# A second layer in column passes of 512 and 256 instead of 384 and 384, and more of the output stored in whole rows

## The chip, the core and the metric

The kernel runs on one core of a Trainium2 chip. The core has a matrix engine (TensorE, "PE" in the profile, with its weight loads as "PEld"), a vector engine (VectorE, "DVE"), an activation engine (ScalarE, "ACT"), a general engine (GpSimd, "POOL"), and SyncE ("SP"), whose queue issues all DMA transfers here. Sixteen DMA engines carry them. PE writes its results into PSUM; ACT or DVE copies them to SBUF; DMA moves SBUF to and from HBM. The metric is the device time of one execution in microseconds (us): 370.72 us before the change, the median of three runs (370.67 to 371.68).

## What is computed

Attention with a sigmoid in place of a softmax, for 8 batches, 12 heads, 448 tokens and head size 64, and behind it a soft mixture of experts on the 3584 tokens x 768 columns that come out (all float32):

```
attn = sigmoid(q k^T / 8 - log 448);  x = (attn v), heads side by side          # 3584 x 768
logits = x phi                                                                  # 3584 x 32 slots
d = softmax over the tokens;  slot_input = d^T x                                # 32 x 768, 4 slots for each of 8 experts
h = max(slot_input[e] w1[e], 0);  slot_out[e] = h w2[e]                         # w1: 8 x 768 x 1024, w2: 8 x 1024 x 768
c = softmax over the slots;  out = c slot_out                                   # 3584 x 768
```

w1 and w2 are 25.2 MB each, the output is 11.0 MB. The change concerns the last two lines only: the second layer (w2), the combination with c, and the stores of the output.

## The kernel before, in words

**Attention and slots.** The first part runs over batches and pairs of heads, with the weights' first units loaded beside it. It ends with the slot inputs (`sT`). Tokens of each batch may be held in another order on the chip: `token_of` (L819) says which token stands at which place, and the queries are permuted on the host by it. Output rows are then stored in that order.

**Weights.** w1 and w2 lie in HBM as 128 units of 128 partitions x 768 columns (0.39 MB each): units 0 to 63 are w1, 64 to 127 are w2. `load_unit`, `load_units` and `load_pair` bring units 0 to 71; `reload` (L128) brings units 72 to 127 into buffers that have become free: `reload(i)` for i from 0 to 9 loads four units with one DMA into `wq0` to `wq9` (units 72+4i to 75+4i), `reload(11)` three into `wa`, `reload(12)` four and then three into `y1`, `reload(13)` three behind `yw[1]`, `reload(14)` two and then one into `xv`. They are called in that order, two behind each expert's first layer (`w1_part`, L669), and all are issued on SP's queue ahead of every store. `units` and `utile` say which tile holds which unit.

**Second layer.** It goes over the output columns in two passes (`hf`), 384 columns (`HALF`) each. One pass has 16 steps (`w2_step`, L775, two for each expert), each with four matmuls of [128 x 32]^T by [128 x 384] into four column groups of PE, all accumulated in one PSUM tile `po`. A unit holds two such blocks of 384 columns; so pass 0 reads w2 units 0 to 31 (units 64 to 95) and pass 1 reads w2 units 32 to 63 (units 96 to 127). Before each expert's two steps GpSimd copies its h into a zeroed buffer (L780). Between the steps of pass 0 stands the softmax over the slots (`combine`, L683).

**Combination.** After a pass `gather` (L758) copies the four partial sums from PSUM in two parts, `spread_sum` (L764) adds them up with a matmul by a constant matrix and copies the sum (`st`), and `out_job` (L710) multiplies it with c. The 28 row blocks of 128 tokens are divided in eight jobs of four and three blocks: job k does blocks of batch pair r = k//2. Each block is a matmul [32 x 128]^T by [32 x 384] (L729; up to four blocks at once in the four row groups of PE), and a copy to SBUF by ACT or DVE in turn (L740). PE's order is written out by hand: in pass 1, `spread_sum` of pass 0 stands before step 3, and out job n-4 before step n, for n = 4 to 11 (L808 to 813). After pass 1, gather, spread and all eight jobs follow for the second half of the columns, in the order 2, 3, ..., 7, 0, 1.

**Stores.** Of the 28 blocks, 16 are stored in two parts, after each pass its 384 columns (rows of 1.5 KB; L743 and L746, five DMAs after each pass); 12 are stored after the second pass in whole rows, two tokens on one partition (6 KB; L751, six DMAs). The staging tiles are `wq` buffers that the first pass has used up.

Of the kernel before, what the change touches and what calls it, by code (L numbers as in the profile page):

```python
# [9 lines left out]
F32 = mybir.dt.float32  # L10
# [14 lines left out]
NPR = H // 2  # L25
NKC = DM // P
NFC = F // P
HALF = DM // 2
UNIT = 768
N_Q = 10  # L30
N_B = 15
N_1 = 4 * N_Q + 17 + N_B
N_T = 4 * N_Q + 3
W_X = N_1 - N_B
NCH = 7
QW = 2 * S
NP = B * NPR
WARM = 6
# [3 lines left out]
BLK = 32  # L42
# [23 lines left out]
def soft_moe_attention(ctx: ExitStack, tc: tile.TileContext, qk, v, vl, phi, wu, wd, wq, wt, cst, out):  # L66
    nc = tc.nc
    ctx.enter_context(tc.manual_schedule(engines=MANUAL))

    wpa = ctx.enter_context(tc.tile_pool(name="wpa", bufs=1))  # L70
    small = ctx.enter_context(tc.tile_pool(name="small", bufs=1))

    places, k = {}, 0
    for name, w in (("cst", 2 * P), ("bias", 1), ("mz", 3), ("rz", 1), ("sm", SLN + 2 * T1),
                    ("phi", NKC * NSLOT), ("lt", B // 2 * NCH * BLK)):
        places[name] = slice(k, k + w)
        k += w
# [9 lines left out]
    nc.vector.memset(nbias, -math.log(S))  # L87

    units = [("w1", e, q, kh) for e in range(E) for kh in range(2) for q in range(4)]
    units += [("w2", hf, e, g, y) for hf in range(2) for e in range(E) for g in range(2) for y in range(2)]  # L90
    state = {"next": 0, "more": N_1}
    utile = {}
    quads = [wpa.tile([P, 4, UNIT], F32, name=f"wq{i}") for i in range(N_Q)]
# [2 lines left out]
    qx = wpa.tile([P, 3, UNIT], F32, name="qx")  # L96
    yt = [wpa.tile([P, 2, 4, TR, NCH, BLK], F32, name=f"y{i}") for i in range(2)]
    yw = {}

    def late_unit(k):  # L100
        return wpb.tile([P, UNIT], F32, name=f"wb{k}")[:]

    def load_units(ns, dst):
        for k, n in enumerate(ns):
            t = wb[n - W_X - 3] if dst is None else dst[:, k, :]
            nc.sync.dma_start(t, wu[n])
            utile[units[n]] = t
# [20 lines left out]
    def reload(i):  # L128
# [31 lines left out]
    with ExitStack() as actx:  # L160
# [12 lines left out]
        first = [("qk", 1), ("qk", 2), ("vl", ""), ("v", 1), ("att0", ""), ("att1", ""), ("xy", "")]  # L173
# [358 lines left out]
        for r in range(NP // 2):  # L532
            p = 2 * r
# [20 lines left out]
        for q, bs in enumerate(jobs):  # L554
            u = (bs[-1] + 1) * per_b + LAG
# [4 lines left out]
            if bs[-1] >= B - 3:  # L560
                k = bs[-1] - B + 3
                at(late, u + 2, lambda k=k: take_y(k))
                n = N_T + 4 + 3 * k
                for i, w in enumerate(((4, 8, 12), (2, 3, 5))[k]):
                    at(late, u + w, lambda k=k, n=n + i, i=i: load_units([n], yw[k][:, 4 + i:5 + i, :]))
            rate.update({u - 2: 1, u - 1: 1, u: 0, u + 1: 0, u + 2: 1, u + 3: 1.2, u + 5: 0.6, u + 6: 1.2})
        for i in range(2):
            at(late, u + 6 + 2 * i, lambda i=i: load_units([N_1 - 2 + i], yw[1][:, 2 + i:3 + i, :]))
        at(late, u + SLOT_AT - 1, lambda: load_units(range(N_1 - 4 - N_B, N_1 - 1 - N_B), xv[:, 0:3, :]))
        at(late, u + SLOT_AT, lambda: slot_job(len(jobs) - 1))  # L570
        at(late, u + SLOT_AT + 1, lambda: load_units(range(4 * N_Q, 4 * N_Q + 4), yw[0][:, 0:4, :]))
# [2 lines left out]
        i = seq.index((NP - 2, NFK - 1)) + LAG  # L574
# [5 lines left out]
        todo = deque()  # L580
# [10 lines left out]
        for i in range(len(seq) + LAG):  # L591
            for f in early.get(i, ()):
                f()
            if i < len(seq):
                u = seq[i]
# [26 lines left out]
            if i >= LAG:  # L622
                u = seq[i - LAG]
# [5 lines left out]
                p, c = u  # L629
# [20 lines left out]

    wpb = ctx.enter_context(tc.tile_pool(name="wpb", bufs=1, reuse_waits="tile"))
    hc = sm[:, 0:E * 32].rearrange("p (e f s) -> p e f s", e=E, f=NFC)
    tmp = sm[:, E * 32:E * 32 + HALF]
    ps_t = ctx.enter_context(tc.tile_pool(name="ps_t", bufs=4, space=PSUM, reuse_waits="tile"))
    ps_h = ctx.enter_context(tc.tile_pool(name="ps_h", bufs=1, space=PSUM, reuse_waits="tile"))
    ps_o = ctx.enter_context(tc.tile_pool(name="ps_o", bufs=2, space=PSUM, reuse_waits="tile"))
# [50 lines left out]
    def psum(n):  # L707
        return ps_t.tile([P, 512], F32, name="pt") if n % 3 else ph_tile(n // 3 + 1)

    def out_job(k, hf):  # L710
        r, o = divmod(k, 2)
        if o == 0 and r == 0:
            w = wpa.tile([P, 4 * UNIT], F32, name=f"wq{8 * hf}")
            halves[0] = w[:, 0:NCH * HALF].rearrange("p (j c) -> p j c", j=NCH)
        elif o == 0:
            if hf == 0:
                rows[r] = wpa.tile([P, 4, UNIT], F32, name=f"wq{r}")
            if r < 3:
                state["wh"] = wpa.tile([P, 2, 2 * UNIT], F32, name=f"wq{4 + 2 * hf + r // 2}")
            halves[r] = state["wh"][:, r % 2, 0:3 * HALF].rearrange("p (j c) -> p j c", j=3)  # L720
        hc = slice(hf * HALF, (hf + 1) * HALF)
        copies = (nc.scalar.copy, nc.vector.tensor_copy)
        todo = []
        for c in range(4 * o, 4 + 3 * o):
            pf = psum(state["out"])
            state["out"] += 1
            n = NCH * r + c
            g = slice(32 * (n % 4), 32 * (n % 4) + 32)
            nc.tensor.matmul(  # L729
                pf[:, 0:HALF], flat[g, P * (n // 4):P * (n // 4 + 1)], sts[hf][g, :], start=True, stop=True)  # L730
            todo.append((c, pf))
        t0 = NCH * P * r
        for i, (c, pf) in enumerate(todo):
            if r == 0:
                ov = halves[0][:, c, :]
            elif 2 <= c < 5:
                ov = halves[r][:, c - 2, :]
            else:
                ov = rows[r][:, c if c < 2 else c - 3, hc]
            copies[i % 2](ov, pf[:, 0:HALF])  # L740
            if r == 0 and c in (3, 6):
                j = slice(0, 4) if c == 3 else slice(4, 7)
                nc.sync.dma_start(  # L743
                    out[j.start * P:j.stop * P, hc].rearrange("(j p) c -> p j c", p=P), halves[0][:, j, :])
            elif r and c == 4:
                nc.sync.dma_start(  # L746
                    out[t0 + 2 * P:t0 + 5 * P, hc].rearrange("(j p) c -> p j c", p=P), halves[r])
            elif r and hf == 1 and c in (1, 6):
                j = 0 if c == 1 else 2
                to = t0 + (0 if c == 1 else 5 * P)  # L750
                nc.sync.dma_start(  # L751
                    out[to:to + 2 * P, :].rearrange("(p k) c -> p k c", k=2), rows[r][:, j:j + 2, :])

    cms, sts, rows, halves = {}, [], {}, {}
    spare = phi_flat
    state["out"] = 0

    def gather(po):  # L758
        so = tmp
        nc.scalar.copy(so[:, 0:HALF // 2], po[:, 0:HALF // 2])  # L760
        nc.scalar.copy(so[:, HALF // 2:], po[:, HALF // 2:HALF])
        return so

    def spread_sum(so):  # L764
        if not sts:
            state["st"] = late_unit(1)
        st = state["st"][:, len(sts) * HALF:(len(sts) + 1) * HALF]
        for k, copy in enumerate((nc.scalar.copy, nc.vector.tensor_copy)):
            c = slice(k * HALF // 2, (k + 1) * HALF // 2)
            pr = ps_t.tile([P, 512], F32, name="pt")  # L770
            nc.tensor.matmul(pr[:, 0:HALF // 2], rep, so[:, c], start=True, stop=True)  # L771
            copy(st[:, c], pr[:, 0:HALF // 2])  # L772
        sts.append(st)

    def w2_step(po, hf, n):  # L775
        e, g = divmod(n, 2)
        h = hw[e % 2]
        if g == 0:
            o = NSLOT - SPE
            nc.gpsimd.tensor_copy(  # L780
                h[:, o:o + NFC * NSLOT].rearrange("p (f s) -> p f s", f=NFC)[:, :, 0:SPE], hc[:, e])
        for fl in range(4):
            k = (4 * g + fl) * NSLOT + NSLOT - SPE - SPE * e
            ut = utile[("w2", hf, e, g, fl // 2)][:, fl % 2 * HALF:(fl % 2 + 1) * HALF]
            nc.tensor.matmul(  # L785
                po[32 * fl:32 * fl + 32, 0:HALF], h[:, k:k + NSLOT], ut,
                start=(n == 0), stop=(n == 2 * E - 1))

    prev = (0, ph)
# [35 lines left out]


# [43 lines left out]
```

## Time and profile before

| | |
|---|---|
| device time, median of 3 runs | 370.72 us (370.67 to 371.68) |
| profiled execution: span, first to last instruction | 369.5 us (no other time of it is given; the median lies 1.2 us above its span) |
| PE busy | 345.6 us, 94% of the span |
| DVE, ACT busy | 214.2 us, 217.9 us |
| mean DMA rate | 258 GB/s over the span, 95.25 MB |
| HBM written | 11.01 MB |
| chain that ended last | PE 81%, DMA 13% of the span |

The time is that of the whole execution; the profile shows one execution with an instruction-by-instruction record. The shares are averages over stages with different limits, so the stage in which the change lies, the last 70 us or so, has to be read by itself: which engine is busy there, which transfers are under way, and who waits for whom. Times within the span count from its start. A DMA's "time to landing" runs from its issue on SP's queue to its end.

### The profile page before, as it was taken

The numbers are of one execution on the slowest core, as the hardware profiler recorded it, in microseconds if no ns is written. First come the engines' busy times: TensorE is split into PE (matmuls) and PEld (weight loads), VectorE is DVE, ScalarE is ACT, GpSimd is POOL, SyncE is SP. The second block draws the span as 40 slices with busy tenths as digits, with TensorE's granted clock in tenths as the row PEclk, the third lists the DMA queues.
The fourth block names the chain that finished last, engine by engine and source line by source line (L and its number), as shares of the span: only waits on it lengthen the run. The fifth ranks groups of instructions, "written<-read, shape, count | busy, mean of one in ns | idle before, by whom it ended". The sixth has DMA issues, their size and how long they took to land.

```text
span 369.5 us, 9946 instructions
## 1 busy us (share of the span) xinstructions
PE 345.6 (94%) x4167; PEld 161.8 (44%) x4167; DVE 214.2 (58%) x482; ACT 217.9 (59%) x294; POOL 5.1 (1%) x24
## 2 busy tenths in 40 slices
PE   9999999999999999999999999999999979997810
PEld 5455555533343354434333633453457643322600
DVE  0155849199764926995764499969855344141510
ACT  5777777587777765777777487747673001142610
POOL 0000000000000000000000000000000001100000
PEclk9999999999999999999999999999999998999975
DMA  7675766667766683676767176429999999999997
GB/s 244 219 225 188 256 219 228 191 184 223 227 210 233 196 271 88 212 233 221 236 217 222 36 227 201 130 64 309 335 317 327 431 421 426 423 419 407 393 407 296
DMA packets 35548, 95.25 MB, mean 258 GB/s; under 512 B 3760, under 2 KB 17712, under 8 KB 33712
## 3 DMA queue, kind: packets, MB, share of 16 engines
q1 hardware_dynamic: 35504, 94.62, 73.2%
q8 instruction: 33, 0.54, 0.6%
q14 instruction: 11, 0.09, 0.1%
HBM read 83.59 MB, written 11.01 MB: 256 GB/s over the span
## 4 chain that ended last, share of the span: by engine, by line
PE 81%; DMA 13%; ACT 0%; DVE 0%; issue 0%; ACTq 0%
PE sc L237 35%; PE av L286 33%; DMA wq<-in_wq_dram 7%; DMA xv<-in_wt_dram 6%; PE sc L329 3%; PE sc L402 2%; PE pt L729 2%; PE ph L155 1%; PE av L155 1%; PE av L527 1%; PE av L266 1%; PE av L409 0%; PE ph L729 0%; PE pt L771 0%; PE po L785 0%; PE av L319 0%
## 5 line engine op out<-in xcount | busy, mean ns | idle before, releaser
L244 ACT ACTIVATE att<-sc,keep 128x896 f32<-128x896 f32 (+1 forms) x167 | 167.4, 1003 | 69.0 <-PE sc L237 64.4
L237 PE MATMUL sc<-qk 64*64 64x448 f32 x896 | 114.5, 536 | 0.0
L303 DVE STREAM_TRANSPOSE y<-xv 32x384 f32<-32x384 f32 (+5 forms) x144 | 69.2, 481 | 2.4
L286 PE MATMUL av<-att,xv 64*64 64x448 f32 x576 | 69.1, 536 | 0.0
L286 PE MATMUL av<-att,v 64*64 64x448 f32 x552 | 65.9, 536 | 0.0
L237 PEld LDWEIGHTS sc<-qk 64*64 64x64 f32 x896 | 41.3, 133 | 45.2 <-issue 18.7
L237 PE MATMUL sc<-qx 64*64 64x448 f32 (+1 forms) x448 | 60.4, 538 | 0.0
L303 DVE STREAM_TRANSPOSE y<-qx 32x288 f32<-32x288 f32 (+5 forms) x80 | 36.0, 450 | 1.3
L286 PEld LDWEIGHTS av<-att,xv 64*64 64x64 f32 x576 | 21.7, 131 | 32.7 <-ACT att L244 30.0
L293 DVE TENSOR_TENSOR xv<-xv,av 128x448 f32<-128x448 f32 x24 | 14.9, 621 | 35.6 <-ACT xv L289 17.6
L286 PEld LDWEIGHTS av<-att,v 64*64 64x64 f32 x552 | 20.5, 131 | 31.3 <-ACT att L244 30.7
L237 PEld LDWEIGHTS sc<-qx 64*64 64x64 f32 x448 | 20.8, 136 | 21.5 <-issue 10.0
L303 DVE STREAM_TRANSPOSE y<-xy 32x288 f32<-32x288 f32 (+1 forms) x48 | 24.9, 519 | 0.7
L286 PE MATMUL av<-att,vl 64*64 64x448 f32 x188 | 22.9, 537 | 0.0
L293 DVE TENSOR_TENSOR qx<-qx,av 128x448 f32<-128x448 f32 x12 | 7.5, 621 | 17.1 <-PE av L286 14.9
L293 DVE TENSOR_TENSOR xy<-xy,av 128x448 f32<-128x448 f32 x11 | 6.8, 622 | 16.6 <-ACT xy L289 14.3
L729 PE MATMUL pt<-wb,keep 32*128 32x384 f32 x74 | 15.3, 531 | 0.5 <-DVE wb L772 0.5
L785 PE MATMUL po<-wq,wb 128*32 128x384 f32 x160 | 14.7, 490 | 0.8 <-DMA wq<-in_wq_dram 0.7
L681 ACT COPY keep<-keep 128x32 f32<-128x32 f32 x8 | 1.8, 225 | 22.2 <-DVE keep L679 16.4
L740 DVE COPY wq<-pt 128x384 f32<-128x384 f32 x16 | 8.6, 555 | 8.9 <-PE ph L729 3.6
L740 ACT COPY wq<-pt 128x384 f32<-128x384 f32 x21 | 9.7, 484 | 6.8 <-PE pt L729 4.8
L289 ACT COPY xv<-av 128x448 f32<-128x448 f32 x24 | 12.6, 524 | 0.0
(150 smaller groups left out, 258.1 us busy)
## 6 DMA issues: line engine op xcount, KB each, us to landing
wq<-in_wu_dram SPq DMA_DIRECT2D x40, 384.0 KB, 4.4
wq<-in_wq_dram SPq DMA_DIRECT2D x10, 1536.0 KB, 21.1
qk<-in_qk_dram SPq DMA_DIRECT2D x32, 448.0 KB, 3.8
qx<-in_qk_dram SPq DMA_DIRECT2D x15, 448.0 KB, 3.4
out_dram<-wq SPq DMA_DIRECT2D x8, 768.0 KB, 8.8
y<-in_wu_dram SPq DMA_DIRECT2D x14, 384.0 KB, 5.4
xv<-in_v_dram SPq DMA_DIRECT2D x24, 192.0 KB, 3.8
v<-in_v_dram SPq DMA_DIRECT2D x24, 192.0 KB, 3.6
```

The lines of the kernel that those rows point to most:

```text
L155: nc.tensor.matmul(ph[32 * j:32 * j + 32, 0:256], sT[:, kc, :], utile[("w1", e, j, kh)][:, kc % 3 * 256:(kc % 3 + 1) * 256], start=(kc == ...
L237: nc.tensor.matmul(banks[h][64 * t:64 * t + 64, tok], qkts[pt][r, S + k0:S + k0 + 64], qkts[pt][r, tok], start=True, stop=True)
L244: nc.scalar.activation(att[:, h, tok], sc[..., tok], AF.Sigmoid, bias=nbias, scale=QSCALE)
L286: nc.tensor.matmul(o[t][r, 0:S], w, att[row, h, :], start=start, stop=stop)
L289: nc.scalar.copy(x_of(p), avs[p][1][:, 0:S])
L293: nc.vector.tensor_tensor(out=x_of(p), in0=x_of(p), in1=av[0][:, 0:S], op=ALU.add)
L303: nc.vector.transpose(y[32 * g:32 * g + 32, a, k0:k0 + n, cy:cy + m, :], src)
L329: nc.tensor.matmul(lg[32 * j:32 * j + 32, b % 2, cols(b, j)], phi_sb[:, hp, :], blocks(x_of(b * NPR + hp), b, j), start=(hp == first), sto ...
L402: nc.tensor.matmul(sl[32 * a:32 * a + 32, 0:SLN], zt[:, c * BLK:(c + 1) * BLK], y[:, :, a, :, c, :], start=(c == 0), stop=(c == n - 1))
L729: nc.tensor.matmul(pf[:, 0:HALF], flat[g, P * (n // 4):P * (n // 4 + 1)], sts[hf][g, :], start=True, stop=True)
L740: copies[i % 2](ov, pf[:, 0:HALF])
L785: nc.tensor.matmul(po[32 * fl:32 * fl + 32, 0:HALF], h[:, k:k + NSLOT], ut, start=(n == 0), stop=(n == 2 * E - 1))
```

## The change

The second layer's columns are taken in passes of 512 and 256 (`GCOLS`). w2 is laid out on the host so that the blocks of 512 columns of all 16 steps come first, without a gap, and the blocks of 256 after them; units, DMAs and buffers stay as they were. The first pass then reads w2 units 0 to 42 and two thirds, the second the rest; `w2_chunk` finds the block in the loaded pieces. There are nine jobs: jobs 0, 1 and 2 (4, 3 and 3 blocks: batch pair 0, and the middle block of the other three pairs) are stored in two parts, after each pass its columns (rows of 2 KB and of 1 KB); jobs 3 to 8 (three blocks each) are stored after the second pass in whole rows, three tokens on one partition (9 KB). In the second pass out job n-4 stands before step n for n = 4 to 12. After the second pass the jobs go in the order 3, ..., 8, 0, 1, 2. The gathered sum goes to a buffer that held weights (`late_unit(2)`). Two weight units are loaded in one place of the attention loop instead of two places.

```
-HALF = DM // 2
+NCH = 7
+NARROW = 3
+JOBS = [range(4), range(4, NCH), range(NCH + 3, 4 * NCH, NCH)]
+JOBS += [range(NCH * r + c, NCH * r + c + 3) for r in range(1, B // 2) for c in (0, 4)]
+GCOLS = (slice(0, 512), slice(512, DM))
...
+    def hold_units(n, t):
+        m = t.shape[1]
+        if n >= n_1:
+            pieces.append((UNIT * (n - n_1), UNIT * m, t.rearrange("p u w -> p (u w)")))
+        for k in range(min(m, n_1 - n)):
+            utile[units[n + k]] = t[:, k, :]
+
+    def w2_chunk(cg, i):
+        w = GCOLS[cg].stop - GCOLS[cg].start
+        at = 64 * GCOLS[cg].start + w * i
+        for first, size, t in pieces:
+            if first <= at and at + w <= first + size:
+                return t[:, at - first:at - first + w]
...
-        for i in range(2):
-            at(late, u + 6 + 2 * i, lambda i=i: load_units([N_1 - 2 + i], yw[1][:, 2 + i:3 + i, :]))
+        at(late, u + 7, lambda: load_units(range(N_1 - 2, N_1), yw[1][:, 2:4, :]))
...
-    def out_job(k, hf):
...
+    def staging(i):
+        return wpa.tile([P, 4, UNIT], F32, name=f"wq{i}")[:].rearrange("p u w -> p (u w)")
+
+    def out_job(k, cg):
+        cs = GCOLS[cg]
+        w = cs.stop - cs.start
+        if k >= NARROW:
+            if cg == 0:
+                rows[k] = staging((1, 2, 3, 5, 6, 7)[k - NARROW])[:, 0:3 * DM].rearrange("p (j c) -> p j c", j=3)
+            to = rows[k][:, :, cs]
+        else:
+            if cg == 0 and k < 2:
+                state["half"] = staging(4 * k)
+            elif cg and k == 0:
+                state["half"] = staging(8)
+            j = (0, 0, 3)[k] if cg == 0 else (0, 4, 7)[k]
+            to = state["half"][:, j * w:(j + len(JOBS[k])) * w].rearrange("p (j c) -> p j c", c=w)
         copies = (nc.scalar.copy, nc.vector.tensor_copy)
         todo = []
+        for n in JOBS[k]:
             pf = psum(state["out"])
             state["out"] += 1
             g = slice(32 * (n % 4), 32 * (n % 4) + 32)
             nc.tensor.matmul(
+                pf[:, 0:w], flat[g, P * (n // 4):P * (n // 4 + 1)], sts[cg][g, :], start=True, stop=True)
+            todo.append(pf)
+        for j, pf in enumerate(todo):
+            copies[j % 2](to[:, j, :], pf[:, 0:w])
+        n = JOBS[k][0]
+        if k >= NARROW:
+            if cg:
+                nc.sync.dma_start(out[n * P:(n + 3) * P, :].rearrange("(p j) c -> p j c", j=3), rows[k])
+        elif k == 2:
+            nc.sync.dma_start(out.rearrange("(r q) c -> q r c", r=B // 2)[3 * P:4 * P, 1:, cs], to)
+        else:
+            nc.sync.dma_start(out[n * P:(n + len(todo)) * P, cs].rearrange("(j p) c -> p j c", p=P), to)
...
-            ut = utile[("w2", hf, e, g, fl // 2)][:, fl % 2 * HALF:(fl % 2 + 1) * HALF]
+            ut = w2_chunk(cg, 4 * n + fl)
...
-    so = gather(po)
+    so = gather(po, 512)
     po = ps_o.tile([P, 512], F32, name="po")
     for n in range(2 * E):
         if n == 3:
-            spread_sum(so)
-        if 4 <= n < 4 + B:
+            spread_sum(so, 0)
+        if 4 <= n < 4 + len(JOBS):
             out_job(n - 4, 0)
         w2_step(po, 1, n)
-    spread_sum(gather(po))
-    for b in range(B):
-        out_job((b + 2) % B, 1)
+    spread_sum(gather(po, DM - 512), 1)
+    for k in range(len(JOBS)):
+        out_job((k + NARROW) % len(JOBS), 1)
```

## Rows read from the trace of the kernel before

**Rows 1.** Windows: us, engines' busy time, granted PE clock, DMA share, GB/s.
```profile
309.00:319.00 10.00, 10.00 (x123) 3.96 (x115) 1.76 (x5) 2.08 (x5) 1.48 (x7) 1.00 1.01 426
363.50:367.00 3.50, 0.00 (x0) 0.00 (x0) 0.00 (x0) 0.00 (x0) 0.00 (x0) 0.50 1.03 381
367.00:368.00 1.00, 0.00 (x0) 0.00 (x0) 0.00 (x0) 0.00 (x0) 0.00 (x0) 0.50 0.22 78
```

**Rows 2.** Chain that ended last: start, us, engine or transfer (x pieces).
```profile
319.44 22.25 DMA xv<-in_wt_dram
341.74 0.86 PE po L785 x4
```

**Rows 3.** Timeline, second pass on PE and PEld: start, us, instruction [idle before <-releaser].
```profile
320.34 0.92 PE L771 MATMUL pt<-keep 128*128 128x192 f32 x4
321.19 0.85 PE L785 MATMUL po<-wq,wb 128*32 128x384 f32 x8
321.97 0.58 PE L729 MATMUL ph<-wb,keep 32*128 32x384 f32 x1
323.24 0.85 PE L785 MATMUL po<-wq,wb 128*32 128x384 f32 x8 [0.34 <-DMA wq<-in_wq_dram]
326.95 0.85 PE L785 MATMUL po<-wq,wb 128*32 128x384 f32 x8 [0.36 <-DMA wq<-in_wq_dram]
328.58 0.85 PE L785 MATMUL po<-wq,wb 128*32 128x384 f32 x8
329.37 0.58 PE L729 MATMUL av<-wb,keep 32*128 32x384 f32 x1
330.22 0.85 PE L785 MATMUL po<-wa,wb 128*32 128x384 f32 x8
338.93 1.49 PE L785 MATMUL po<-y,wb 128*32 128x384 f32 x12 [0.83 <-DMA y<-in_wt_dram]
340.77 1.81 PE L785 MATMUL po<-xv,wb 128*32 128x384 f32 x12 [0.36 <-DMA xv<-in_wt_dram]
```

**Rows 4.** DMA packets: 309:319, 338:339, 339:340, 340:341, 341:342, 342:346, 346:347.
```profile
DMA packets 389, 4.26 MB, mean 426 GB/s; under 512 B 43, under 2 KB 43, under 8 KB 43
DMA packets 137, 0.40 MB, mean 401 GB/s; under 512 B 13, under 2 KB 62, under 8 KB 136
DMA packets 194, 0.40 MB, mean 396 GB/s; under 512 B 8, under 2 KB 146, under 8 KB 194
DMA packets 247, 0.40 MB, mean 398 GB/s; under 512 B 12, under 2 KB 225, under 8 KB 247
DMA packets 267, 0.40 MB, mean 398 GB/s; under 512 B 10, under 2 KB 265, under 8 KB 267
DMA packets 1082, 1.60 MB, mean 400 GB/s; under 512 B 41, under 2 KB 1082, under 8 KB 1082
DMA packets 216, 0.33 MB, mean 333 GB/s; under 512 B 14, under 2 KB 211, under 8 KB 216
```

**Rows 5.** Timeline from the second pass's end to the first store after it.
```profile
342.68 0.32 ACT L760 COPY keep<-po 128x192 f32<-128x192 f32 x1 [5.12 <-PE po L785]
344.01 0.36 DVE L772 COPY wb<-pt 128x192 f32<-128x192 f32 x1 [6.71 <-PE pt L771]
345.43 0.48 ACT L740 COPY wq<-pt 128x384 f32<-128x384 f32 x1 [1.43 <-PE pt L729]
345.47 1.02 DVE L740 COPY wq<-pt 128x384 f32<-128x384 f32 x2 [1.10 <-PE pt L729]
346.09 0.34 SPq L751 DMA_DIRECT2D out_dram<-wq  x1
```

**Rows 6.** Groups by line and shape: the copy of 512 columns by ACT.
```profile
L705 ACT COPY keep<-pt 128x512 f32<-128x512 f32 x1 | 0.6, 587 | 3.6 <-PE pt L704 3.6
```

**Rows 7.** Wait at the start of the second layer, and the stretch behind it (as Rows 1).
```profile
304.62 0.98 PE L785 MATMUL po<-wp,wb 128*32 128x384 f32 x8 [2.02 <-POOL wb L780]
305.30:308.70 3.40, 3.40 (x28) 1.24 (x24) 2.62 (x7) 0.58 (x1) 0.21 (x1) 0.51 1.02 430
```

More of the change, by code (lines that the diff above doesn't have):

```diff
@@ L34 @@
 W_X = N_1 - N_B
-NCH = 7
 QW = 2 * S
@@ L89, in soft_moe_attention @@
     units = [("w1", e, q, kh) for e in range(E) for kh in range(2) for q in range(4)]
-    units += [("w2", hf, e, g, y) for hf in range(2) for e in range(E) for g in range(2) for y in range(2)]
+    n_1 = len(units)
+    pieces = []
     state = {"next": 0, "more": N_1}
@@ L106, in load_units @@
             nc.sync.dma_start(t, wu[n])
-            utile[units[n]] = t
+            if n < n_1:
+                utile[units[n]] = t
+        if ns[0] >= n_1:
+            hold_units(ns[0], dst)
     def load_unit():
@@ L118, in load_pair @@
         nc.sync.dma_start(t, wd[(n - W_X - 7) // 4])
-        for k in range(2):
-            utile[units[n + k]] = t[:, k, :]
+        hold_units(n, t)
     def load_many(src, t):
         nc.sync.dma_start(t, src)
-        for k in range(t.shape[1]):
-            utile[units[state["more"] + k]] = t[:, k, :]
+        hold_units(state["more"], t)
         state["more"] += t.shape[1]
@@ L652, in soft_moe_attention @@
     hc = sm[:, 0:E * 32].rearrange("p (e f s) -> p e f s", e=E, f=NFC)
-    tmp = sm[:, E * 32:E * 32 + HALF]
+    tmp = sm[:, E * 32:E * 32 + 256]
     ps_t = ctx.enter_context(tc.tile_pool(name="ps_t", bufs=4, space=PSUM, reuse_waits="tile"))
@@ L708, in psum @@
         return ps_t.tile([P, 512], F32, name="pt") if n % 3 else ph_tile(n // 3 + 1)
-    def out_job(k, hf):
[L711 to L721, printed above, removed]
+    def staging(i):
+        return wpa.tile([P, 4, UNIT], F32, name=f"wq{i}")[:].rearrange("p u w -> p (u w)")
@@ L722, in out_job @@
         copies = (nc.scalar.copy, nc.vector.tensor_copy)
         todo = []
-        for c in range(4 * o, 4 + 3 * o):
+        for n in JOBS[k]:
             pf = psum(state["out"])
             state["out"] += 1
-            n = NCH * r + c
             g = slice(32 * (n % 4), 32 * (n % 4) + 32)
             nc.tensor.matmul(
-                pf[:, 0:HALF], flat[g, P * (n // 4):P * (n // 4 + 1)], sts[hf][g, :], start=True, stop=True)
-            todo.append((c, pf))
-        t0 = NCH * P * r
@@ L733, in out_job @@
[L733 to L752, printed above, removed]
@@ L754, in soft_moe_attention @@
-    cms, sts, rows, halves = {}, [], {}, {}
+                pf[:, 0:w], flat[g, P * (n // 4):P * (n // 4 + 1)], sts[cg][g, :], start=True, stop=True)
[10 more added lines that the diff above has]
+            nc.sync.dma_start(out[n * P:(n + len(todo)) * P, cs].rearrange("(j p) c -> p j c", p=P), to)
@@ L755, in soft_moe_attention, with gather, spread_sum @@
+    cms, sts, rows = {}, [], {}
     spare = phi_flat
     state["out"] = 0
[L758 to L761, printed above, removed]
+    def gather(po, w):
+        so = late_unit(2)[:, 0:w]
+        for c in (slice(0, w // 2), slice(w // 2, w)):
+            nc.scalar.copy(so[:, c], po[:, c])
         return so
-    def spread_sum(so):
+    def spread_sum(so, cg):
         if not sts:
@@ L766, in spread_sum @@
             state["st"] = late_unit(1)
-        st = state["st"][:, len(sts) * HALF:(len(sts) + 1) * HALF]
+        st = state["st"][:, GCOLS[cg]]
+        w = so.shape[1] // 2
         for k, copy in enumerate((nc.scalar.copy, nc.vector.tensor_copy)):
-            c = slice(k * HALF // 2, (k + 1) * HALF // 2)
+            c = slice(k * w, (k + 1) * w)
             pr = ps_t.tile([P, 512], F32, name="pt")
-            nc.tensor.matmul(pr[:, 0:HALF // 2], rep, so[:, c], start=True, stop=True)
-            copy(st[:, c], pr[:, 0:HALF // 2])
+            nc.tensor.matmul(pr[:, 0:w], rep, so[:, c], start=True, stop=True)
+            copy(st[:, c], pr[:, 0:w])
@@ L773, in spread_sum, with w2_step @@
         sts.append(st)
-    def w2_step(po, hf, n):
+    def w2_step(po, cg, n):
         e, g = divmod(n, 2)
@@ L783, in w2_step @@
             k = (4 * g + fl) * NSLOT + NSLOT - SPE - SPE * e
-            ut = utile[("w2", hf, e, g, fl // 2)][:, fl % 2 * HALF:(fl % 2 + 1) * HALF]
+            ut = w2_chunk(cg, 4 * n + fl)
             nc.tensor.matmul(
-                po[32 * fl:32 * fl + 32, 0:HALF], h[:, k:k + NSLOT], ut,
+                po[32 * fl:32 * fl + 32, 0:ut.shape[1]], h[:, k:k + NSLOT], ut,
                 start=(n == 0), stop=(n == 2 * E - 1))
@@ L809, in soft_moe_attention @@
         if n == 3:
-            spread_sum(so)
-        if 4 <= n < 4 + B:
+            spread_sum(so, 0)
+        if 4 <= n < 4 + len(JOBS):
             out_job(n - 4, 0)
         w2_step(po, 1, n)
-    spread_sum(gather(po))
-    for b in range(B):
-        out_job((b + 2) % B, 1)
+    spread_sum(gather(po, DM - 512), 1)
+    for k in range(len(JOBS)):
+        out_job((k + NARROW) % len(JOBS), 1)
 def token_of(b, i):
-    if b < 2:
-        return i
-    if b % 2 == 0:
-        return 2 * (i % P) + i // P if i < 2 * P else i
-    return i if i < S - 2 * P else S - 2 * P + 2 * ((i - S) % P) + (i - S) // P + 2
+    first = 64 * (b % 2)
+    if b < 2 or not first <= i < first + 3 * P:
+        return i
+    return first + 3 * ((i - first) % P) + (i - first) // P
 def kernel(**inputs):
@@ L843 @@
     w1 = inputs["moe_w1"].reshape(E, 2, TR, P, 4, 256).transpose(0, 1, 4, 3, 2, 5).reshape(E, 2, 4, P, UNIT)
-    w2 = inputs["moe_w2"].reshape(E, 4, 2, 2, 2, BLK, 2, HALF).transpose(6, 0, 2, 3, 1, 5, 4, 7)
-    w2 = w2.reshape(2, E, 2, 2, P, UNIT)
-    w = np.concatenate([w1.reshape(-1, P, UNIT), w2.reshape(-1, P, UNIT)])
+    w2 = inputs["moe_w2"].reshape(E, 4, NFC, BLK, DM).transpose(1, 3, 0, 2, 4).reshape(P, E * NFC, DM)
+    w2 = np.concatenate([w2[:, :, cs].reshape(P, -1) for cs in GCOLS], axis=1)
+    w2 = w2.reshape(P, -1, UNIT).transpose(1, 0, 2)
+    w = np.concatenate([w1.reshape(-1, P, UNIT), w2])
     nt = N_1 + 4 * N_Q
```

## The prediction

> **What bounds the kernel now.** I read the chain of waits first. Its last long pieces are transfers: the w2 load into `wq7` lands at 319.44, the last w2 load at 341.74 [rows 2]; behind that only one step of matmuls, the combination and the stores are left. Then the windows, to see whether these transfers wait for anything. The reader is to see a DMA share of 1.0 all through the loads, 426 GB/s, and about 381 to 400 GB/s while the stores drain, up to 367, where the rate falls to 78 [rows 1, 4]. So from the loads on the 16 DMA engines never rest, but for one place: 333 GB/s in 346 to 347 [rows 4], which is where the first store of the second pass (issued at 346.09 [rows 5]) comes just too late for the engines that are ahead. The last 28 us are a drain of 11.01 MB, and whoever empties its queue pays.
>
> Last the timeline of PE in the second pass. A step stands every 1.64 us (328.58 to 330.22), of which 0.79 is the step and 0.85 the out job behind it [rows 3]. PE is ahead of the loads: it waits for `wq8` at 323.24, for `wq9` at 326.95, and again at 338.93, 340.77 and for the last load at 341.74 [rows 2, 3]. It has some 1 to 3 us in hand, and this slack is what the change spends.
>
> **The change part by part.** The sums are made in the profiled execution's time (span 369.5; the median of the runs, 370.72, lies 1.2 above it, and I add the same 1.2 at the end).
>
> *Loads.* The same units, DMAs, buffers and order on SP; none waits for a tile of the second layer. The two units loaded at one place of the attention loop change the place of one load by a step, long before the drain. Cost 0. The bounds: nothing waits for them sooner, so no gain; if they stood in front of a transfer that PE waits for, 0.79 MB at 426 GB/s, 1.8 us of loss. I take 0, since no row of the drain has to do with them. The last load stays at 341.74.
>
> *First pass, 512 columns.* A step costs 0.64 us of columns now (0.85 less the 0.2 until the last result), so 512 columns cost 0.85. But the pass now needs w2 units up to 42.67, so its last step (blocks 60 to 63) needs `wq8`, and the second pass from its step 1 on (block 4 onward) needs `wq9`. So the pass ends at 323.24 + 0.85 + 0.2 = 324.3 (now the pass and three steps of the next are done by 320.34 [rows 3]), and step 1 of the second pass stands at 326.95, when `wq9` is there, however fast PE is. Behind that wait on PE stand the spread and all out jobs, and for these wait ACT and DVE with the copies and SP with the stores. The staging tiles, the other new dependence, are no wait: `wq0` to `wq7` are read by then, `wq8` before step 1.
>
> *Out jobs begin later.* `spread_sum` is behind step 2 as before. Step 1 at 326.95; step 2 at 327.38 (256 columns are 0.43); spread at +0.55 (0.43 and the 0.12 between), 327.93. Spread to step 3 was 0.85 for four pieces of 192 [rows 3], 0.64 of it columns; of 256 it is 0.85 + 0.21 = 1.06, so step 3 is at 329.0 and out job 0 at 329.0 + 0.57 = 329.56. It was at 321.97 [rows 3]: 7.6 us later, against the same last load.
>
> *And they are nine, not eight.* Job and step together were 768 columns twice and are 768 columns twice, 512 + 256: 1.28 us of columns and 0.36 of gaps. The gaps I take as they are: 1.64. Bounds: 1.28, no gaps at all, and 2.0, if three matmuls in PE's row groups overlap worse than four (now they don't: the job between 326.95 and 328.58 has three blocks, the one at 329.37 four, and the pairs take 1.63 and 1.64 [rows 3]). Copies do not hold it up: ACT needs 0.587 for 512 columns [rows 6], two in a job, 1.2 of 1.64 us. Step 12 then stands at 329.56 + 8 x 1.64 + 1.06 = 343.7, step 15 at 343.7 + 3 x 0.43 = 345.0, and its result is there at 345.0 + 0.43 + 0.2 = 345.6. By the loads alone it could end at 342.4. The second pass has become bound by PE, by 3.2 us.
>
> *From there to the first store.* Now: 342.58 to 346.09 = 3.5 us (gather, spread, first matmuls, copies [rows 5]). The pieces are 128 wide instead of 192 and 256 instead of 384: two gather and two spread copies 0.05 each, spread's columns 0.2, the job's columns 0.2; the DMA now needs three blocks instead of two, +0.06. Sum 3.5 - 0.5 = 3.0, bounds 2.4 (all by columns) and 3.5. The store is issued at 348.6 and its packets run 0.8 later (issued at 346.09, five packets of over 2 KB began before 347 [rows 4]), at 349.4.
>
> *The queue in front of it shrinks.* First what a packet costs. With only 1.5 KB packets, 342 to 346, 1041 data packets (1082 less 41) took 4 us of 16 engines, 61.5 ns each; 12 KB loads 10 x 16 / 346 = 462 ns [rows 4]. The line through both: 4.3 ns a packet and 37.2 ns a KB (1000 B). So 2 KB is 80.5 ns, 1 KB 42.4, 6 KB 233, 9 KB 347. Bounds for 1 KB: 38 (by bytes at 426 GB/s) and 64 (as much as a 1.5 KB packet at 381 GB/s [rows 1]); for 9 KB: 346 and 387 (by bytes at 381). After the first pass each engine held 16 blocks x 8 = 128 packets of 1.5 KB, 7.9 us. It will hold 80 of 2 KB, 6.4 us. The engines come to the stores between 338 and 341.7: of some 260 packets a us the share of 1.5 KB is 19%, 53%, 82%, 98% in the four windows from 338 [rows 4], on the mean 339.5. So they run dry between 344.6 and 348.1, mean 345.9, and the next store comes at 349.4. The mean engine rests 3.5 us, the slowest one 1.3.
>
> *The last drain.* Each engine has 6 jobs x 8 = 48 packets of 9 KB, 16.7 us, and 80 of 1 KB, 3.4: 20.1, with the ends of the bounds 19.6 to 23.7. I take the line through the packets: 9 KB is nearest to the 12 KB row, 1 KB to that of 1.5 KB at 400 GB/s. The same sum for the kernel before, from 339.5: 128 x 2 x 61.5 ns + 48 x 233 = 26.9, so 366.4, where 367.2 is read [rows 1]: 2 to 3% too little, part of it the rest at 346. With 2%, 20.1 is 20.5. The drain ends at 369.9, 2.7 after the 367.2 of before; counted by the slowest engine, 1.3 of rest less the 0.4 saved in packets (96 an engine x 4.3 ns), plus that 2%, some 1.4 later. All engines start together then, so the lag among them is less than now; I take 2.2 of these 1.4 to 2.7. Twelve stores instead of sixteen on SP's queue free nothing that anyone waits for.
>
> Sum: 370.72 + 2.2 = 372.9.
>
> For small transfers the Trainium skill (Perfetto Trace Analysis, DMA Optimizations) says that those under 2 KB carry a significant cost each. The trace: 1.5 KB packets at 400 GB/s against 426 for 12 KB [rows 4], 6%. By the rule the new 1 KB packets, 80 an engine, would stand near the dear end, 64 ns: 1.7 us more.
>
> **The rivals.**
>
> *PE's clock halves (B).* After the change PE rests twice: for about a us before 323.24 (PE is through with the first pass's other steps some 15 x 0.21 = 3.2 us later than now) and from about 324.6 to 326.95. Before, a rest of 2.02 us at 304.62 was followed by 3.4 us at a granted clock of 0.51, 1.2 instead of 2.4 GHz [rows 7]; the rests at 338.93 (0.83 us) and 340.77 (0.36) were not [rows 3]. If it falls after the second rest, steps 1 to 3 and the spread (2.1 us of columns) take up to 1.7 us more, and all behind them. Time 372.9 + 0.9 to 1.7: 373.8 to 374.6. On this the Trainium skill (TensorE: Matmul & The Clock Gate, Part 1) says that half speed is the default and activity lifts it; by that rule rests in the second pass are what to fear, and rows 7 agree.
>
> *Small packets are dear (E).* 64 ns for 1 KB adds 80 x 21.6 = 1.7 us: 374.6. Against it: the step from 12 KB to 1.5 KB cost 6% only.
>
> *The queue never runs dry where it counts (C), not slower.* The end is set by the last engine. It has stores up to 348.1. If the first packet of the next store is there by then, it loses nothing, and the end is that of before less 0.4: 370.3. It decides at a second pass that ends by 344.3, that is nine pairs of job and step at 1.49 us instead of 1.64. For it: the gaps (0.36 a pair) may be shorter with longer matmuls. Against it: they were the same in every pair that did not wait, of three and of four blocks.
>
> *The packets saved are worth more (D), faster.* As C, and with 381 instead of 400 GB/s for 1.5 KB packets, 64.5 ns, the fixed part is 7.7 ns, so 96 x 7.7 = 0.7 us, and whole rows at 430 GB/s another 0.3 to 0.5: 369.5. It needs C first.
>
> **How the numbers follow.** Chances: forecast 0.50, B 0.18, E 0.09, C 0.16, D 0.07. The likeliest one's own range is 371.5 to 374.0 (the slowest engine's 1.4 less 0.6 for a shorter chain of 2.4, to the mean's 2.7 with 0.6 of dear packets). The range over the cases goes from 370.1, which takes in C, to 374.6, which takes in most of B and E; D and some of the upper ends are left out. A measurement of this kernel can tell about 0.3%, 1.1 us, from no change, so slower is above 371.8 and faster below 369.6. Slower: B and E, 0.27, and 0.46 of the forecast's 0.50, 0.73. Same: C, 0.16, and the low end of the forecast, 0.04: 0.20. Faster: D, 0.07.
>
> **What would show it.** The load into `wq9` still lands near 326.85 and the last one near 341.74, so PE's wait for `wq9` stands before step 1, not before step 6. Out job 0 stands at 329.6, pairs of job and step 1.64 us apart, and no step from 7 on waits for a DMA. The gather of the second pass waits for PE at about 345.6, the first 9 KB store is issued at about 348.6. DMA share falls to about half or less between 346 and 349.4; from there on it is 1.0 at 400 to 425 GB/s. Wrong would be: no such hole, or PE still waiting for the last load; then C holds. A granted clock of 0.5 between 323 and 330 is B; under 370 GB/s in the last 3 us is E.

## The result and the profile after

The kernel after takes 375.08 us (median of six runs, 373.28 to 376.49), the kernel before beside it 371.33: a ratio of 1.0098, with a 95% interval of 1.0073 to 1.0123. Run again beside other experiments it gave 1.0107 (1.0076 to 1.0138). The change makes the kernel 1% slower. The forecast was 372.9, which is 1.0059 times the 370.72 known then, with a range to 374.6, and 375.08 lies above it: the side was right, the size too small.

The profiled execution of the kernel after has a span of 371.4 us, 1.9 more than before, and is the shortest of its six runs; the others have spans of 372.2 to 374.7. Both the part of the cost that this profile shows and the part that it lacks are needed.

First the timeline of PE in the second layer of this execution (start, us, instruction, idle time and its releaser):

```profile
318.37 1.05 PE L797 MATMUL po<-wq,wb 128*32 128x512 f32 x4 [1.13 <-DMA wq<-in_wq_dram]
...
322.06 1.50 PE L797 MATMUL po<-wq,wb 128*32 128x512 f32 x16 [1.05 <-DMA wq<-in_wq_dram]
325.76 1.07 PE L797 MATMUL po<-wq,wb 128*32 128x256 f32 x16 [2.20 <-DMA wq<-in_wq_dram]
326.76 1.13 PE L783 MATMUL pt<-wb,keep 128*128 128x256 f32 x4
327.82 0.64 PE L797 MATMUL po<-wq,wb 128*32 128x256 f32 x8
...
334.58 0.64 PE L797 MATMUL po<-y,wb 128*32 128x256 f32 x8
...
336.21 0.64 PE L797 MATMUL po<-y,wb 128*32 128x256 f32 x8
...
343.44 1.24 PE L797 MATMUL po<-xv,wb 128*32 128x256 f32 x17
```

Where [rows 3] had the spread at 320.34, three waits for loads come first: 1.13 us within the first pass, 1.05 for `wq8` before its last step, 2.20 for `wq9` before step 1 of the second. The spread follows at 326.76. From there on a step comes every 1.63 us (334.58 to 336.21), and no step waits for a DMA any more; before, the last loads were waited for [rows 3]. PE ends the second pass at 344.68 (343.44 + 1.24) instead of 342.58. Then the way to the first store, as [rows 5]:

```profile
344.80 0.43 ACT L772 COPY wb<-po 128x128 f32<-128x128 f32 x2 [0.89 <-PE po L797]
...
345.87 0.29 DVE L784 COPY wb<-pt 128x128 f32<-128x128 f32 x1 [2.29 <-PE pt L783]
...
347.01 0.37 ACT L755 COPY wq<-pt 128x256 f32<-128x256 f32 x1 [1.10 <-PE ph L751]
...
347.68 0.34 SPq L759 DMA_DIRECT2D out_dram<-wq  x1
```

It takes 3.0 us (3.5 before), so the store is issued 1.6 us later than before. What this does to the DMA engines stands in the windows (as Rows 1: us, busy time of the engines, granted PE clock, DMA share, GB/s):

```profile
338.00:344.00 6.00, 6.00 (x66) 2.04 (x63) 2.75 (x4) 4.24 (x8) 0.42 (x2) 1.00 1.04 405
344.00:345.00 1.00, 0.68 (x16) 0.13 (x4) 0.00 (x0) 0.20 (x2) 0.00 (x0) 1.00 0.90 346
345.00:346.00 1.00, 0.71 (x4) 0.52 (x4) 0.13 (x1) 0.50 (x3) 0.00 (x0) 1.00 0.59 227
346.00:347.00 1.00, 0.69 (x9) 0.72 (x12) 0.16 (x1) 0.00 (x0) 0.00 (x0) 1.00 0.09 35
347.00:348.00 1.00, 1.00 (x14) 0.61 (x11) 0.85 (x2) 0.99 (x4) 0.00 (x0) 1.00 0.00 0
348.00:351.00 3.00, 3.00 (x36) 2.90 (x31) 2.01 (x5) 3.00 (x11) 0.00 (x0) 1.00 0.83 337
344.00:352.00 8.00, 7.08 (x76) 5.68 (x64) 3.93 (x10) 5.55 (x19) 0.00 (x0) 1.00 0.64 257
...
366.00:369.00 3.00, 0.00 (x0) 0.00 (x0) 0.00 (x0) 0.00 (x0) 0.00 (x0) 0.50 1.04 348
```

The queue that the first pass left is empty between 344 and 347, and in 347 to 348 nothing moves at all. Before, the same place had one window at 333 GB/s [rows 4]. Against 400 GB/s the four windows from 344 lack (54 + 173 + 365 + 400) / 400 = 2.5 us of transfer, and the stretch from 344 to 352 as a whole, at 257 GB/s, lacks 8 x (400 - 257) / 400 = 2.9 us. The drain behind it is that of the new stores; the packet counts give their prices (windows 342 to 344 with 2 KB packets alone, 358 to 362 with 9 KB, 366 to 369 with 1 KB):

```profile
DMA packets 415, 0.82 MB, mean 409 GB/s; under 512 B 16, under 2 KB 16, under 8 KB 415
DMA packets 200, 1.69 MB, mean 422 GB/s; under 512 B 17, under 2 KB 17, under 8 KB 17
DMA packets 1036, 1.04 MB, mean 348 GB/s; under 512 B 32, under 2 KB 1034, under 8 KB 1034
```

Without those under 512 B, 399 packets of 2 KB in 2 us of 16 engines are 80 ns each, 183 of 9 KB in 4 us 350 ns, 1002 of 1 KB in 3 us 48 ns.

### The profile page after: what moved, and what is told of

It reads as the page before. It is cut to its first block, busy times and chain, and to the rows that moved or that the text cites. A ratio compares the mean times of both kernels' runs of the same rounds, so it can differ in the third digit from the quotient of the medians.

```text
span 371.4 us, 9929 instructions
## 1 busy us (share of the span) xinstructions
PE 343.3 (92%) x4167; PEld 160.0 (43%) x4167; DVE 212.6 (57%) x478; ACT 219.6 (59%) x298; POOL 5.1 (1%) x24
## 4 chain that ended last, share of the span: by engine, by line
PE 82%; DMA 12%; ACT 0%; SPq 0%; issue 0%; DVE 0%; ACTq 0%
PE sc L256 34%; PE av L305 33%; DMA wq<-in_wq_dram 11%; PE pt L751 3%; PE sc L348 3%; PE sc L421 2%; PE po L797 2%; DMA qx<-in_qk_dram 1%; PE av L174 1%; PE av L285 1%; PE ph L751 0%; PE pt L783 0%; PE av L428 0%; PE av L751 0%; PE av L256 0%
## 5 line engine op out<-in xcount | busy, mean ns | idle before, releaser
L797 PE MATMUL po<-wq,wb 128*32 128x512 f32 (+1 forms) x136 | 15.1, 546 | 4.4 <-DMA wq<-in_wq_dram 4.4
L751 PE MATMUL pt<-wb,keep 32*128 32x256 f32 (+1 forms) x74 | 16.0, 524 | 0.5 <-DVE wb L784 0.5
L755 DVE COPY wq<-pt 128x512 f32<-128x512 f32 (+1 forms) x17 | 9.5, 566 | 10.4 <-PE av L751 5.2
L755 ACT COPY wq<-pt 128x256 f32<-128x256 f32 (+1 forms) x20 | 9.3, 470 | 5.9 <-PE ph L751 2.8
```

What stands on the lines that cost most here:

```text
L751: nc.tensor.matmul(pf[:, 0:w], flat[g, P * (n // 4):P * (n // 4 + 1)], sts[cg][g, :], start=True, stop=True)
L755: copies[j % 2](to[:, j, :], pf[:, 0:w])
L797: nc.tensor.matmul(po[32 * fl:32 * fl + 32, 0:ut.shape[1]], h[:, k:k + NSLOT], ut, start=(n == 0), stop=(n == 2 * E - 1))
```

## The experiments

The theory after this profile (A): the out jobs begin behind the load into `wq9`, PE ends the second pass late, and because the first pass leaves a shorter queue, the DMA engines rest. It explains the 1.9 us of the profiled execution. What was open: why the other runs are longer still. The mean granted clock of the runs gave a lead: 0.978 in the profiled one, 0.973 or 0.974 in the five others.

**e1 and e6: PE kept busy in its waits.**

```
+    def keep_busy(m):
+        pd = ps_t.tile([P, 512], F32, name="pt")
+        for _ in range(m):
+            nc.tensor.matmul(pd[:, 0:WN], zero, zero, start=True, stop=True)
+    keep_busy(8)                       # ahead of the first pass
...
+        if n in (13, 15):
+            keep_busy(4)               # first pass
...
+        if n == 1:
+            keep_busy(9)               # second pass
```

> The kernel after, with small matmuls of a constant zero put on PE (into a PSUM tile that nobody reads) where it waits: 8 before the first pass, 4 before its steps 13 and 15, 9 before step 1 of the second pass. Theory A (the timed runs are 1 to 3 us longer than the profiled one because PE's clock falls to half during those waits in most executions): every run is like the profiled one, a mean clock near 0.978 or above, span 371.0 to 371.8, about 1.006 times the kernel before. Rival (the spread of the runs comes from the transfers, or the clock does not matter): the runs stay at 374 to 376, 1.010 times the kernel before, whatever the clock.

> The kernel after with PE kept busy in its waits, as e1, once more beside e5 on the same chip. Clock theory: median 1 to 2 us below that of e5 (ratio 1.005 to 1.007 against 1.009 to 1.011) with mean clocks of 0.976 or more. Transfer theory: the same median as e5.

Measured: 1.0068 (1.0042 to 1.0094) and 1.0052 (1.0036 to 1.0069). The second was run on the same chip as the unchanged kernel after (e5, 1.0107): medians 373.28 and 375.65 us. The intervals of these two do not touch; that of e1 overlaps with the one of the first measurement (1.0073 to 1.0123). The mean clocks are 0.976 to 0.981 in all 19 runs. PE's order of useful work is the same, so 1 to 2.4 us of the cost is what becomes of PE in its waits, and 2 to 2.5 us stay. Not every run of e1 is like the profiled one, as was expected: one has a span of 373.9 at a clock of 0.979, and this length is not the clock's. In e1 the matmuls fill the wait for `wq9` (PE's timeline; step 1 follows them without a rest, and they may hold it up by some tenths):

```profile
323.81 2.27 PE L816 MATMUL pt<-const-float32-0.0 128*128 128x128 f32 x18
326.08 1.07 PE L797 MATMUL po<-wq,wb 128*32 128x256 f32 x16
```

In e6 step 1 and the first store of the second pass stand at:

```profile
326.92 1.07 PE L797 MATMUL po<-wq,wb 128*32 128x256 f32 x16
...
348.85 0.34 SPq L759 DMA_DIRECT2D out_dram<-wq  x1
```

**e5 and e8: the kernel after again.**

> The kernel after, unchanged, beside e6 on one chip. What is open is why its timed runs (spans 372.2 to 374.7) are longer than the profiled one (371.4). Clock theory: most executions have one more stretch of 3.4 us at half speed between 318 and 330, where PE rests for w2 loads; the runs with a mean clock of 0.973 or 0.974 are then the longer ones, the median is 374 to 375, and a profile that shows such a stretch shows the second pass ending 1 to 2 us later than 344.7. Transfer theory: lengths do not go with the clock, and a long run shows slow loads or a slow drain instead.

> The kernel after once more, one look with a profile, to catch an execution with a half-speed stretch in the second layer. Clock theory: where the granted clock is 0.5 in some stretch between 318 and 330, the pairs of job and step in it are about 3 us instead of 1.63 apart, and the first store of the second pass is issued as much later as PE lost; without such a stretch the span is near 371.4. Transfer theory: no such link.

Measured: e5 1.0107, spans 372.3 to 374.9 at mean clocks of 0.969 to 0.975; e8 a span of 374.1 at 0.968. Both profiles show what the first one lacks. Windows of e5, around the wait for `wq9` and behind it:

```profile
325.00:327.10 2.10, 0.00 (x0) 0.00 (x0) 0.00 (x0) 0.26 (x1) 0.00 (x0) 1.00 1.01 423
327.70:331.00 3.30, 3.30 (x20) 1.50 (x16) 0.26 (x1) 0.37 (x1) 0.21 (x1) 0.50 1.01 426
331.00:335.00 4.00, 4.00 (x41) 1.28 (x36) 2.15 (x4) 1.90 (x4) 0.21 (x1) 0.99 1.00 420
```

Its timeline in the same place, and its first store of the second pass:

```profile
327.16 1.54 PE L797 MATMUL po<-wq,wb 128*32 128x256 f32 x16 [2.19 <-DMA wq<-in_wq_dram]
328.63 2.08 PE L783 MATMUL pt<-wb,keep 128*128 128x256 f32 x4
330.63 0.81 PE L797 MATMUL po<-wq,wb 128*32 128x256 f32 x8
...
346.35 1.24 PE L797 MATMUL po<-xv,wb 128*32 128x256 f32 x17
...
350.59 0.34 SPq L759 DMA_DIRECT2D out_dram<-wq  x1
```

Behind the rest of 2.19 us PE's granted clock is 0.50, the 1.2 of its two levels of 1.2 and 2.4 GHz. The spread takes 2.08 us instead of 1.13; from the wait's end to step 3 it is 3.47 us instead of 2.06. The same stretch in e8, with its step 1 and its first store, and in the kernel after's first profile:

```profile
326.40:329.80 3.40, 3.27 (x19) 1.77 (x20) 0.00 (x0) 0.15 (x1) 0.21 (x1) 0.50 1.02 431
```

```profile
326.53 1.93 PE L797 MATMUL po<-wq,wb 128*32 128x256 f32 x16 [2.20 <-DMA wq<-in_wq_dram]
...
349.99 0.34 SPq L759 DMA_DIRECT2D out_dram<-wq  x1
```

```profile
326.40:329.80 3.40, 3.36 (x32) 1.33 (x28) 0.56 (x2) 0.55 (x2) 0.42 (x2) 1.00 1.01 428
```

So the first store of e5 comes 2.9 us later than in the first profile (350.59 to 347.68): 1.4 because `wq9` landed later in that execution (327.16 to 325.76), 1.4 by the half speed up to step 3, 0.1 behind it. The late landing and the clock can be told apart: from the start of step 1 to the first store it is 21.9 us where PE is at full speed (first profile, e1, e6) and 23.4 and 23.5 us where it is not (e5, e8). In e6 step 1 starts later than in e8, and its store comes 1.1 us earlier. The hole in the stores follows (windows from 344 to 352, e6 and e8):

```profile
344.00:352.00 8.00, 7.08 (x83) 5.47 (x84) 3.67 (x9) 5.59 (x19) 0.00 (x0) 1.00 0.56 222
344.00:352.00 8.00, 7.08 (x76) 4.78 (x73) 2.92 (x7) 4.76 (x15) 0.21 (x1) 0.89 0.39 151
```

Counted as before, these 8 us lack 3.6 us of transfer in e6 and 5.0 in e8. (The 0.89 of e8 is one more stretch at half speed, from 350 on, behind its first store.)

Some expectations were missed. The median of e5 is 375.65 and not 374 to 375. Its second pass ends at 347.59, 2.9 us later than in the first profile and not 1 to 2, because its loads were late too. The half-speed stretch lies over steps 1 to 3 and the spread, not over pairs of job and step, which stay 1.63 us apart. And length does not follow the mean clock run by run within e5: 372.3 at 0.973, 374.2 at 0.969, 374.9 at 0.973. The mean does not say where PE was slow. The kernel before has its half-speed stretch behind the rest of 2.02 us before the first pass [rows 7], where it delays no store; the same rest in the kernel after is followed by full speed in all three profiles. In the first of them:

```profile
305.30:308.70 3.40, 3.40 (x36) 1.04 (x32) 2.62 (x6) 0.58 (x1) 0.42 (x2) 1.00 1.02 430
```

In e3 (below) it is as in the kernel before: 0.51 there, and full speed behind a rest of 2.21 us before step 1; its mean clock is 0.974. No profile has both stretches. So the stretch behind the wait for `wq9` is shown in two of the three profiles of the kernel after. That most of its other runs have it is argued from e1 and e6; what decides where it comes, and what else spreads the runs, is open.

**e2: the rows alone.** Nine jobs and whole rows of three tokens, both passes 384 columns.

```
-GCOLS = (slice(0, 512), slice(512, DM))
+GCOLS = (slice(0, DM // 2), slice(DM // 2, DM))
...
-            elif cg and k == 0:
-                state["half"] = staging(8)
-            j = (0, 0, 3)[k] if cg == 0 else (0, 4, 7)[k]
+            elif cg and k != 1:
+                state["half"] = staging(8 + k // 2)
+            j = (0, 0, 3)[k] if cg == 0 else (0, 4, 0)[k]
...
```

> The new row layout and nine jobs alone; both passes 384 columns. Theory A (what costs is that the out jobs begin behind the load into wq9, so that PE ends the second pass late and the store queue runs dry): out job 0 is back near 322, the second pass ends with the last load near 342.5, the first 9 KB store is issued near 346; the queue in front of it is shorter (80 packets of 1.5 KB an engine, 4.9 us, dry between 343 and 346.6), so a small hole stays: 1.002 to 1.005 times before. Rival P (the cost lies in the new stores themselves, their whole rows of 9 KB or the job order): near the kernel after, 1.008 to 1.012.

Measured: 1.0026 (1.0009 to 1.0044). The stores alone cost a quarter of the whole. There is a hole too, earlier and for the other reason: PE is in time, with the first store at 345.94 (346.09 before), but the queue of 80 packets of 1.5 KB is too short (store and windows):

```profile
345.94 0.34 SPq L759 DMA_DIRECT2D out_dram<-wq  x1
344.00:345.00 1.00, 0.86 (x9) 0.70 (x12) 0.00 (x0) 0.00 (x0) 0.00 (x0) 1.00 0.41 154
345.00:346.00 1.00, 1.00 (x12) 0.50 (x8) 0.81 (x2) 0.95 (x3) 0.00 (x0) 1.00 0.20 62
...
347.00:348.00 1.00, 1.00 (x11) 0.82 (x10) 0.77 (x2) 1.00 (x4) 0.00 (x0) 1.00 1.07 442
```

**e3: the columns alone.** The kernel before with passes of 512 and 256 columns (the layout of w2, `w2_chunk`, `gather`, `spread_sum` and the place of the two weight units as in the kernel after); eight jobs, 16 blocks in two parts and rows of two tokens as before; in the first pass the parts lie in `wq0`, `wq4` and `wq5`. Against the kernel before:

```
-HALF = DM // 2
+GCOLS = (slice(0, 512), slice(512, DM))
...
-            ut = utile[("w2", hf, e, g, fl // 2)][:, fl % 2 * HALF:(fl % 2 + 1) * HALF]
+            ut = w2_chunk(hf, 4 * n + fl)
...
```

> The passes of 512 and 256 columns alone; the old eight jobs, 16 blocks in two parts, 12 in rows of two tokens. PE is as late as in the kernel after (out job 0 near 328.5, second pass ending near 343.5, one job less), but the first pass leaves 128 packets of 2 KB an engine in the queue, 10.3 us, up to 349 to 352, and the first store of the second pass comes at about 346.5. Theory A with the queue as the link: no hole, and the time is that of before plus the dearer 1 KB packets, 1.000 to 1.003. Rival Q (a late end of the second pass costs by itself, whatever lies in the queue): 1.006 or more.

Measured: 0.9997 (0.9976 to 1.0019). This is the run that names the link. PE is as late as in the kernel after, and the first store as well (timeline):

```profile
343.42 1.24 PE L816 MATMUL po<-xv,wb 128*32 128x256 f32 x17
...
347.52 0.34 SPq L781 DMA_DIRECT2D out_dram<-wq  x1
```

but 16 blocks of 2 KB rows lie in the queue, and it never runs dry (windows):

```profile
345.00:346.00 1.00, 0.71 (x4) 0.52 (x4) 0.15 (x1) 0.48 (x3) 0.00 (x0) 1.00 1.04 403
346.00:347.00 1.00, 0.71 (x10) 0.74 (x12) 0.14 (x1) 0.01 (x1) 0.00 (x0) 1.00 1.06 412
347.00:348.00 1.00, 1.00 (x12) 0.60 (x10) 0.97 (x3) 0.91 (x3) 0.00 (x0) 1.00 1.04 403
```

A late second pass by itself has no cost clear of the noise here; it costs what the DMA engines rest. Neither part of the change alone has the loss of both: 1.0026 and 0.9997 against 1.0098.

**e4: the out jobs earlier.** PE gets something to do while it waits for `wq9`.

```
-        if n == 3:
+        if n == 1:
             spread_sum(so, 0)
-        if 4 <= n < 4 + len(JOBS):
-            out_job(n - 4, 0)
+        if 1 <= n < 1 + len(JOBS):
+            out_job(n - 1, 0)
```

> The kernel after, with spread_sum before step 1 of the second pass instead of step 3, and out job n-1 before step n instead of job n-4. PE then has the out jobs to do while it waits for wq9. Theory A: out job 0 near 326 instead of 328.5, the second pass ends with the last load near 342.5 instead of 344.7, the first 9 KB store is issued near 345.5 instead of 347.7, the hole in the store queue shrinks from about 3 us to less than 1, and with no wait of 2 us on PE in the second pass its clock stays up: 0.999 to 1.003 times before. Rival P (stores): as the kernel after, 1.008 to 1.012.

Measured: 1.0028 (1.0008 to 1.0047), inside what was expected, though the second pass ended at 343.3 and the store came at 346.29, 0.8 later than expected. Moving three lines takes back 0.7 of the 1.0%. PE's clock stays at 1.00 through the second pass. The hole is smaller, but not under 1 us as expected: the two windows shown lack 1.4 us (windows):

```profile
345.00:346.00 1.00, 1.00 (x12) 0.65 (x12) 0.34 (x1) 0.39 (x2) 0.00 (x0) 1.00 0.42 164
346.00:347.00 1.00, 1.00 (x14) 0.96 (x12) 0.64 (x3) 1.00 (x4) 0.00 (x0) 1.00 0.15 59
```

**e7: early jobs and a longer queue.** On top of e4 one more job of three blocks is stored in two parts; its staging tiles and the order of its tokens change with it.

```
-NARROW = 3
+NARROW = 4
-JOBS = [range(4), range(4, NCH), range(NCH + 3, 4 * NCH, NCH)]
-JOBS += [range(NCH * r + c, NCH * r + c + 3) for r in range(1, B // 2) for c in (0, 4)]
+JOBS = [range(4), range(4, NCH), range(NCH + 3, 4 * NCH, NCH), range(NCH, NCH + 3)]
+JOBS += [range(NCH * r + c, NCH * r + c + 3) for r in range(1, B // 2) for c in (0, 4) if (r, c) != (1, 0)]
...
```

> e4 with a fourth job in two parts (13 blocks in two parts, 15 in whole rows of three tokens): the queue in front of the first whole-row store is 104 packets of 2 KB an engine, 8.4 us instead of 6.4. Theory A (the hole in the store queue is what costs): the hole of about 2.5 us on the mean engine that e4 still has shrinks to under 1 us, and the time is that of before within 0.15%, 0.998 to 1.0015. Rival P (the layout of the stores costs, or the early out jobs do): as e4, 1.002 to 1.004.

Measured: 0.9993 (0.9977 to 1.0008), 370.85 us against 371.18. The hole is one window at 350 GB/s:

```profile
345.00:346.00 1.00, 1.00 (x13) 0.60 (x12) 0.43 (x2) 0.47 (x2) 0.00 (x0) 1.00 1.05 408
346.00:347.00 1.00, 1.00 (x11) 1.00 (x12) 0.60 (x2) 1.00 (x5) 0.00 (x0) 1.00 0.91 350
347.00:348.00 1.00, 1.00 (x14) 0.96 (x12) 0.64 (x3) 1.00 (x5) 0.00 (x0) 1.00 1.16 457
```

With the passes of 512 and 256 and the nine jobs kept, and rows of three tokens in five of the six jobs that had them, the loss is gone. The other layout of one job cannot be the reason: by the prices above, three tokens cost 350 ns as one packet of 9 KB and 3 x (80 + 48) = 384 ns in two parts. It is not shown to be faster than the kernel before.

## Why the prediction was wrong in size

**The loads as a fixed frame: right.** PE waited for `wq9` before step 1 of the second pass and not before step 6, until 325.76 to 327.16 in three profiles, where 326.95 was taken. That it moves by 1.4 us from one execution to the next was not in the sum.

**The late second pass: right.** Pairs of job and step at 1.63 us (1.64 forecast, with the gaps kept), no wait for a load at the end, 3.0 us to the first store (3.0). With `wq9` 1.2 us earlier than assumed, the pass ended 0.9 earlier than the 345.6 of the sum.

**The hole: right.** The engines ran dry between 344 and 347 (forecast 344.6 to 348.1) and lacked 2.9 us (3.5 for the mean engine), and e3 and e7 show that the queue is the link.

**The packets: two right, one too cheap.** 2 KB cost 80 ns (80.5 forecast), 9 KB 350 (347), 1 KB 48 (42.4), so 80 of them cost 0.4 us more. The sign set for rival E, under 370 GB/s in the last 3 us, did show (348 GB/s), but it stood too close to the forecast: E's own price, 64 ns or 1.7 us, was far off. The Trainium skill (Perfetto Trace Analysis, DMA Optimizations) puts a significant cost on transfers under 2 KB; the trace agrees for 1 KB (348 GB/s against 409 for 2 KB) more than the line through 1.5 and 12 KB had it.

**The clock: the step that failed.** The sum took PE at full speed through the second pass, as in the trace of before there, and left the half speed to rival B with a chance of 0.18. The rows for it were at hand: after a rest of 2.02 us PE had gone on at 0.51 [rows 7], and the sum itself made a rest of 2.3 us before step 1. In the profiles of e5 and e8 this happened; in the first profile it did not, behind the same rest. B's price was right: 0.9 to 1.7 us by the forecast, 1.5 in both; its total, 373.8 to 374.6 on 370.72, is a ratio of 1.0083 to 1.0105, and 1.0098 and 1.0107 were measured. And e1 and e6, in which PE does not rest, give 1.0068 and 1.0052, where the sum without B has 1.0059. So the mechanism of the forecast and that of B are both shown; what was wrong is that they were taken as alternatives, with the half speed at nothing in the sum. On this the Trainium skill (TensorE: Matmul & The Clock Gate, Part 1) says that half speed is the default and activity lifts it. The runs agree in part: 0.50 behind rests of 2.2 us in e5 and e8, but 1.00 behind the same rest in the first profile and in e3.

Two parts of the agreement are luck. The 2.2 us of the sum were chosen between 1.4 and 2.7, and in the first profile an early `wq9` more than made up for the dearer 1 KB packets. And the profiled runs of e5 and e8 are 3.5 and 2.7 us longer than the first one, of which B's 1.5 is only a part: `wq9` landed 1.4 and 0.8 us later in them too.

C and D, in which the last engine's queue is never dry, needed a second pass that ends by 344.3. It ended at 344.68 in the earliest of three profiles and at 346.99 and 347.59 in the others.

## What to carry to other kernels

Where the end of a kernel is a drain of DMA queues, ask of each change how much work lies in the queue at the moment when its last input lands, and how long the first new transfer takes from there; here 6.4 us of stores stood against a first store that was issued more than 8 us after the engines, on the mean, had begun them. A column split that moves work behind a later load needs its dependent work moved ahead of the wait, not left at the same step number. When a change gives the matrix engine a new wait, price what comes after the wait at half speed as well, as part of the likeliest case, not beside it; here half speed followed such a wait in two of four profiles (e5 and e8, not the first one and e3).

## What the runs showed of the hardware

The two parts of this change lose 1% together, but 0.26% and nothing clear of the noise alone: the one shortens the store queue, the other delays the store that has to come before it is empty, and both draw on the same slack. And one profiled execution can miss a cost that other executions of the same kernel have: the kernel after's first profile (371.4 us) had PE at full speed from 318 to 350, and the two taken later (374.9 and 374.1) did not. A rest of about 2 us on PE was followed by a stretch at half speed in some executions and not in others: before the first pass in the kernel before and in e3, before step 1 of the second in e5 and e8, at neither place in the kernel after's first profile.
